# PSUM constants, a shared bank for the state product, and spread ordering copies in an attention, routing and expert kernel

## The chip, the cores and the metric

The kernel runs on one core of a Trainium2 chip. The metric is device time in microseconds: the median of three runs before the change is 863.5 us, from 861.35 to 866.65. An execution that the hardware profiler recorded took 862.23 us.

## The reference

Three layers follow one another; the output of each is the input of the next.

```python
# 1: gated linear attention, B=4, heads 8, sequence 768, head size 48
f = 1.0 / (1.0 + np.exp(-f_logit))
for t in range(S):
    state = f[:, :, t, :, None] * state + np.einsum('bhd,bhe->bhde', k[:, :, t], v[:, :, t])
    y[:, :, t] = np.einsum('bhd,bhde->bhe', q[:, :, t], state)
# 2: 3072 tokens x 384; 8 experts, 384 tokens each, given out in order of the logits x @ w_gate
out[mask] = np.maximum(x[mask] @ w1[e], 0.0) @ w2[e]          # F = 1024
# 3: dense layer, 2048 wide
h = x @ w_in
out = (h * np.clip(h + 3.0, 0.0, 6.0) / 6.0) @ w_out
```

The weights w_in and w_out of the third layer arrive as 64-bit floating point numbers; the kernel reads them as pairs of 32-bit words.

## The kernel before, in words

**Attention** runs on 24 chunks of 128 tokens (`NCH`). Three chunks make a unit of 384 tokens (`U`), eight units in all (`NU`). For a unit, the rows of f, k and q are loaded, put in order per head pair by three copies each (`reorder`: f and k on ScalarE, with the tanh in f's copy; q on GpSimd), and transposed on TensorE into one of three PSUM banks `pT` (line 82). ScalarE turns a transposed f into the forget factors `ff` (line 86). VectorE makes from these two running products by scans: P forward (line 94, whose second stream `m0` restarts the product at each chunk) and S backward (line 92). k times S is `kh` (line 99), q times P is `qt` (line 106). The products at chunk ends, held at a least value of 2^-60, are `pc` (line 96).

A unit has twelve such transposed groups (`ORD`, four head pairs times f, k, q). They are made one unit ahead, four in each chunk (`tg(0)` to `tg(3)`), and `group` puts VectorE's work of one group behind that of the group before. The order of all queues is the order in which the loop over j at the end of `attention` issues things; no scheduler moves them. In an iteration the loop issues:

1. `tg(0)`, then the logits and output of the chunk before (`l_mm`, line 196, into the one bank `pM`), one deferred ScalarE copy (`one`), `tg(1)`;
2. the state's part of the output (`y_mm` part 0, line 164), the scores of the next chunk (`a_mm`, line 136, into the banks pA0 and pA1), their two copies out on ScalarE (`a_ev`, line 141) and masks on GpSimd (line 142);
3. the rest of the output (line 170), then the key-value product (`kv_mm`, line 182, into its own bank `pK`), which VectorE adds to the state (line 189) at the end of the next group;
4. `tg(2)`, the transposed keys of the next chunk (`kt_mm`, line 149, into `pM`, copied out on ScalarE at line 150), `tg(3)`.

PSUM has eight banks, all taken: three pT, pA0, pA1, pM, pY, pK. Chunks are counted here by their scores: chunk n begins with the first matmul of line 136 for it.

`refill` is called in each third chunk: for f its three copies are issued at once, for k they go into a list (`byact`), from which `one` takes one at a time.

Between VectorE's steps of a group, the loop takes a step of the preparation of w_in and w_out (`narrowed`): for each piece of 128x512 words, ScalarE takes the absolute high word (line 904), VectorE holds it at a least value of 2^-15 (line 914), shifts it (916), puts in sign and exponent (918) and joins the low word (921, written over the loaded words `pw`). ScalarE rounds the result to the high half `wih` (691), GpSimd subtracts for the low half `wil` (692). A piece two further on is then fetched into the `pw` buffer that this frees.

**Routing and experts.** A search over the logits picks each expert's tokens; its first steps lie among the last chunks. Each expert's 384 tokens go through both later layers in three matmul passes per product (lines 695 to 697). In the last matmuls `l4` of an expert (k is its number, f the slice of 128 of the 2048 hidden values, t one of three groups of 128 tokens) the three results are finished one after the other, scaled on ScalarE (868) and stored by an indirect DMA that GpSimd issues (870).

Of the kernel before, what the change touches and what calls it, by code (L numbers as in the profile page):

```python
# [17 lines left out]
def attention(tc, q,k,v,f,wg, x_dram, lg, ident, pmin, ranges, prep, setup, spin):  # L18
    nc=tc.nc
    ctx=ExitStack()  # L20
    with ctx:
# [10 lines left out]
        m0=cs.tile([128,U],F32,name="m0")  # L32
        nc.vector.memset(m0,0.0)
        nc.vector.memset(m0.rearrange("p (c t) -> p c t",t=C)[:,:,0:1],1.0)
        m1=cs.tile([128,2,U],F32,name="m1"); nc.vector.memset(m1,0.0)
# [33 lines left out]
        def tgroup(u,p,nm):  # L69
# [14 lines left out]
            if nm=='f':  # L84
# [11 lines left out]
                return (ops+[lambda: V.tensor_scalar(PC[u][:,pp],ends(P2),PMIN,None,op0=OP.max)],  # L96
# [46 lines left out]
        def kt_mm(j):  # L143
# [3 lines left out]
            pk=ps.tile([128,NP,128],F32,name="pM",bufs=MB)  # L147
# [26 lines left out]
        def kv_mm(j):  # L174
# [3 lines left out]
            bank=ps.tile([128,512],F32,name="pK")  # L178
            pk=bank[:,:NP*D].rearrange("p (a d) -> p a d",a=NP)
# [12 lines left out]
        def l_mm(j):  # L192
            W=2*D+8
            px=ps.tile([128,512],F32,name="pM" if j<NCH-1 else "pK",bufs=MB)[:,:NP*W].rearrange("p (a e) -> p a e",a=NP)
# [20 lines left out]
        def warm(n):  # L215

            t=ps.tile([128,512],F32,name="pK")
            for _ in range(n): nc.tensor.matmul(t[:,:128],ident,ident,start=True,stop=True)
# [8 lines left out]
        def refill(u,nm):  # L227
            if u<NU:
                if nm=='k':
# [10 lines left out]
        for nm in 'fkq': refill(1,nm)  # L240
        one()
# [4 lines left out]
        for j in range(-1,NCH+1):  # L246
# [11 lines left out]
            one()  # L258
# [3 lines left out]
            if ti==2: refill(tu+1,'f')  # L262
# [6 lines left out]
            if j>=0: kv_mm(j)  # L269
            tg(2)  # L270
            one()
# [3 lines left out]
            if ti==2: refill(tu+1,'k'); one()  # L275
# [59 lines left out]
class Routing:  # L335
# [3 lines left out]
    def constants(s):  # L339
# [36 lines left out]
        G.iota(w,pattern=[[-1,4]],base=4,channel_multiplier=1)  # L376
        nc.vector.tensor_scalar(w,w,3,None,op0=OP.bitwise_and)
# [3 lines left out]
        G.iota(w,pattern=[[-1,128]],base=128,channel_multiplier=1)  # L381
        nc.vector.tensor_scalar(w,w,31,None,op0=OP.bitwise_and)
# [318 lines left out]
class Experts:  # L701
# [90 lines left out]
    def ffn_(s,k):  # L792
# [61 lines left out]
        for f in range(14):  # L854
# [9 lines left out]
        for t in range(3):  # L864
            l4(14,t); yield
# [12 lines left out]
def gla_moe_ffn(tc,q,k,v,f_logit,moe_w_gate,moe_w1,moe_w2,moe2_w_in,moe2_w_out,out):  # L878
    nc=tc.nc
    with ExitStack() as ctx:  # L880
# [9 lines left out]
        def narrowed(pool,jobs,W,work,places,PW=None):  # L890
# [17 lines left out]
            for i in range(len(jobs)):  # L908
                yield
                r=got[i]  # L910
                if words:
                    V=nc.vector
                    lw,hw=got[i][:,:,0],got[i][:,:,1]; m=mag[i]; t=m.bitcast(U32)
                    V.tensor_scalar(m,m,2.0**-15,None,op0=OP.max)
# [6 lines left out]
                    V.scalar_tensor_tensor(lw,lw,29,t,op0=OP.logical_shift_right,op1=OP.bitwise_or)  # L921
                    r=lw.bitcast(F32)
                hi,lo=places(i)
                if W!=DM:
                    split_raw(nc,r,hi,lo,nc.gpsimd)
                    fetch(i+2)
# [47 lines left out]
        def both(*gens):  # L974
            for g in gens: yield from g
# [133 lines left out]
```

## Time and profile before

| | us |
|---|---|
| median of three runs | 863.5 (861.35 to 866.65) |
| the profiled execution | 862.23 |
| its span, first to last instruction | 860.5 |
| TensorE busy (matmuls), share of the span | 816.0, 95% |
| VectorE busy | 564.4, 66% |
| ScalarE busy | 381.4, 44% |
| GpSimd busy | 155.7, 18% |
| attention's last matmuls start | 179.25 |
| last matmul starts | 848.88 |

[...] Where a row names a releaser, the engine was idle before the instruction until that releaser ended. On TensorE neighbouring matmuls overlap, so the pace is read from start to start. Engines: PE is TensorE, PEld its weight loads, DVE VectorE, ACT ScalarE, POOL GpSimd, SP the queue of most DMAs.

### The profile page before, as it was taken

The numbers are of one execution on the slowest core, as the hardware profiler recorded it, in microseconds if no ns is written. First come the engines' busy times: TensorE is split into PE (matmuls) and PEld (weight loads), VectorE is DVE, ScalarE is ACT, GpSimd is POOL, SyncE is SP. The second block draws the span as 40 slices with busy tenths as digits, with TensorE's granted clock in tenths as the row PEclk, the third lists the DMA queues.
The fourth block names the chain that finished last, engine by engine and source line by source line (L and its number), as shares of the span: only waits on it lengthen the run. The fifth ranks groups of instructions, "written<-read, shape, count | busy, mean of one in ns | idle before, by whom it ended". The sixth has DMA issues, their size and how long they took to land.

```text
span 860.5 us, 15930 instructions
## 1 busy us (share of the span) xinstructions
PE 816.0 (95%) x6062; PEld 778.5 (90%) x6062; DVE 564.4 (66%) x1491; ACT 381.4 (44%) x768; POOL 155.7 (18%) x233
## 2 busy tenths in 40 slices
PE   7999899888998899999999999999999999999994
PEld 6878788777987899999999999999999999999994
DVE  7999999767879846855674676657665522642431
ACT  5776677524345424441453254245415432641431
POOL 5665565302000200110101100300110020000001
PEclk9999999996999999999999999999999999999997
DMA  8776776256002301211211121202211230210000
GB/s 240 191 208 174 195 194 162 86 212 211 1 1 74 111 19 62 87 56 37 74 56 53 50 65 47 83 22 71 90 30 47 58 100 1 74 40 26 1 1 32
DMA packets 77157, 71.91 MB, mean 84 GB/s; under 512 B 29200, under 2 KB 65040, under 8 KB 77072
## 3 DMA queue, kind: packets, MB, share of 16 engines
q1 hardware_dynamic: 74000, 61.37, 24.7%
q0 software_dynamic: 3072, 9.44, 3.4%
q8 instruction: 49, 0.80, 0.4%
q14 instruction: 36, 0.29, 0.1%
HBM read 61.35 MB, written 9.44 MB: 82 GB/s over the span
## 4 chain that ended last, share of the span: by engine, by line
PE 54%; DVE 11%; issue 10%; ACT 3%; DMA 1%; POOL 1%; SPq 0%; POOLq 0%; DVEq 0%; ACTq 0%
PE pF L695 9%; PE acc L695 9%; PE pF L696 8%; PE pF L697 8%; PE acc L697 8%; PE acc L696 8%; DVE ga L838 2%; DVE hl L841 2%; ACT hh L840 1%; DVE w1l L744 1%; ACT ga L837 1%; DMA xh<-in_moe_w_dram 1%; POOL out_dram L870 1%; PE pF L782 1%; DVE q_ge L473 1%
## 5 line engine op out<-in xcount | busy, mean ns | idle before, releaser
L838 DVE SCALAR_TENSOR_TENSOR ga<-ga,pF 128x384 f32<-128x384 f32 x128 | 70.8, 553 | 97.5 <-ACT ga L837 97.1
L695 PE MATMUL pF<-xh,wih 128*128 128x384 f32 x384 | 131.0, 341 | 0.0
L696 PE MATMUL pF<-xh,wil 128*128 128x384 f32 x384 | 129.4, 337 | 0.0
L697 PE MATMUL pF<-xl,wih 128*128 128x384 f32 x384 | 129.3, 337 | 0.0
L837 ACT ACTIVATE ga<-pF,three 128x384 f32<-128x384 f32 x128 | 74.3, 580 | 90.7 <-PE pF L697 83.9
L840 ACT CAST hh<-ga 128x384 fp32r<-128x384 f32 x128 | 65.8, 514 | 101.4 <-DVE ga L838 101.4
L695 PE MATMUL acc<-wo,hh 128*128 128x384 f32 x288 | 100.8, 350 | 0.0
L696 PE MATMUL acc<-wo,hl 128*128 128x384 f32 x288 | 97.4, 338 | 0.1
L697 PE MATMUL acc<-wo,hh 128*128 128x384 f32 x288 | 97.4, 338 | 0.0
L870 POOL DMA_INDIRECT out_dram<-ga,q_ids x24 | 23.9, 997 | 395.3 <-ACT ga L868 392.0
L841 DVE TENSOR_TENSOR hl<-ga,hh 128x384 fp32r<-128x384 f32 x128 | 71.3, 557 | 31.2 <-ACT hh L840 28.0
L803 ACT ACTIVATE hh<-pF 128x384 fp32r<-128x384 f32 x64 | 31.5, 492 | 130.3 <-PE pF L697 125.4
L804 DVE SCALAR_TENSOR_TENSOR hl<-pF,hh 128x384 fp32r<-128x384 f32 x64 | 35.5, 555 | 73.8 <-ACT hh L803 73.5
L695 PEld LDWEIGHTS pF<-xh,wih 128*128 128x128 f32 x384 | 72.3, 188 | 0.2 <-issue 0.2
L696 PEld LDWEIGHTS pF<-xh,wil 128*128 128x128 f32 x384 | 72.2, 188 | 0.0
L697 PEld LDWEIGHTS pF<-xl,wih 128*128 128x128 f32 x384 | 72.1, 188 | 0.0
L695 PE MATMUL pF<-xh,w1h 128*128 128x384 f32 x192 | 67.7, 353 | 0.6 <-ACT xh L773 0.6
L695 PE MATMUL acc<-hh,w2h 128*128 128x384 f32 x192 | 65.9, 343 | 0.0
L696 PE MATMUL pF<-xh,w1l 128*128 128x384 f32 x192 | 65.8, 343 | 0.0
L697 PE MATMUL pF<-xl,w1h 128*128 128x384 f32 x192 | 65.7, 342 | 0.0
L697 PE MATMUL acc<-hl,w2h 128*128 128x384 f32 x192 | 64.5, 336 | 0.1
L761 POOL DMA_INDIRECT xg<-x_dram,q_ids x24 | 24.4, 1017 | 220.8 <-PE pF L697 111.5
(303 smaller groups left out, 1839.4 us busy)
## 6 DMA issues: line engine op xcount, KB each, us to landing
wst<-in_moe_w_dram SPq DMA_DIRECT2D x58, 192.0 KB, 2.4
wst<-in_moe_w_dram SPq DMA_DIRECT2D x42, 256.0 KB, 2.7
pw<-in_moe_w_in_dram SPq DMA_DIRECT2D x12, 512.0 KB, 3.8
v<-in_v_dram SPq DMA_DIRECT2D x24, 192.0 KB, 4.8
x_dram<-y SPq DMA_DIRECT2D x24, 192.0 KB, 4.2
wo<-in_moe_w_out_dram SPq DMA_DIRECT2D x12, 384.0 KB, 8.0
fr<-in_f_logit_dram SPq DMA_DIRECT2D x7, 576.0 KB, 5.2
kr<-in_k_dram SPq DMA_DIRECT2D x7, 576.0 KB, 5.5
```

The source lines that it names most:

```text
L473: V.scalar_tensor_tensor(ge[:,c0:c1],x[:,c0:c1,None].to_broadcast([128,c1-c0,32]),base[:,0:1],grid[:,None,:].to_broadcast([128,c1-c0,32]), ...
L695: nc.tensor.matmul(out, ahi, bhi, start=start, stop=False)
L696: nc.tensor.matmul(out, alo, bhi, start=False, stop=False)
L697: nc.tensor.matmul(out, ahi, blo, start=False, stop=stop)
L761: nc.gpsimd.indirect_dma_start(out=xg[:,h],out_offset=None,in_=s.x,in_offset=bass.IndirectOffsetOnAxis(ap=ids[:,h:h+1],axis=0))
L803: nc.scalar.activation(hh,p,AF.Relu)
L804: s.defer(2,lambda: nc.vector.scalar_tensor_tensor(hl,p,0.0,hh.bitcast(F32),op0=OP.max,op1=OP.subtract))
L837: nc.scalar.activation(a,p,AF.Relu,bias=s.three[:,0:1])
L838: late(f,1,lambda: nc.vector.scalar_tensor_tensor(g,a,6.0,p,op0=OP.min,op1=OP.mult))
L840: late(f,1,lambda: nc.scalar.copy(gh,g))
L841: late(f,3,lambda: nc.vector.tensor_tensor(out=gl,in0=g,in1=gh.bitcast(F32),op=OP.subtract))
L870: st=nc.gpsimd.indirect_dma_start(out=s.out,out_offset=bass.IndirectOffsetOnAxis(ap=ids[:,t:t+1],axis=0),in_=o,in_offset=None)
```

## The change

1. The bank `pK` goes to constants (`held`): m0, the least value 2^-60 and the least value 2^-15 lie there in PSUM. The P scan reads m0 from it; the two maxima with a constant become maxima of two tensors, the second a column of the bank read again and again.
2. The key-value product is written into pA0; the warming matmuls at the start into pY; the last chunk's logits into pT. The transposed keys of chunks 22 and 23 go to pT (23 has none).
3. f's three copies are issued one at a time from the second chunk of a unit on, k's copies two at the unit's last chunk and one in the next.
4. A joined word of w_in is written into its scratch `pm` and not over `pw`, and the next fetch is issued ahead of the low half's subtraction.
5. Two constants of the routing are made in two steps, so that VectorE's part is issued an iteration after GpSimd's.
6. In the last expert, f = 13 of the last matmuls moves into the loop over t.

```diff
--- before
+++ after
@@ -29,9 +29,10 @@
             nc.vector.memset(t[:,:,:,:,48:],1.0 if nm=='f' else 0.0)
             perm[nm]=t
         half=cs.tile([128,1],F32,name="half"); nc.vector.memset(half,0.5)
-        m0=cs.tile([128,U],F32,name="m0")
-        nc.vector.memset(m0,0.0)
+        held=ps.tile([128,512],F32,name="pC"); m0=held[:,:U]
+        nc.vector.memset(held[:,:U],0.0); nc.vector.memset(held[:,U:U+1],PMIN); nc.vector.memset(held[:,U+1:],2.0**-15)
         nc.vector.memset(m0.rearrange("p (c t) -> p c t",t=C)[:,:,0:1],1.0)
+        least=held[:,U:U+1,None].to_broadcast([128,2,3]); normal.append(held[:,U+1:U+2])
         m1=cs.tile([128,2,U],F32,name="m1"); nc.vector.memset(m1,0.0)
         SW=cs.tile([128,NP,2*D+8],F32,name="sw"); nc.vector.memset(SW,0.0)
         for s in range(2):
@@ -93,7 +94,7 @@
                 SF[u,p]=suffix
                 ops=[lambda: V.tensor_tensor_scan(P,m0,ff[:,:U],1.0,op0=OP.max,op1=OP.mult)]
                 if p%2==0: return ops,[]
-                return (ops+[lambda: V.tensor_scalar(PC[u][:,pp],ends(P2),PMIN,None,op0=OP.max)],
+                return (ops+[lambda: V.tensor_tensor(out=PC[u][:,pp],in0=ends(P2),in1=least,op=OP.max)],
                         [lambda: V.reciprocal(ends(m1),PC[u][:,pp]),SF[u,p-1]])
             elif nm=='k':
                 return [lambda: nc.vector.tensor_mul(KH[u][:,p],pf,SS[u,p])],[]
@@ -144,7 +145,8 @@
             u,c=divmod(j,3)
             if j%6==5: return
             kt=wk.tile([128,4,2,64],F32,name="kt")
-            pk=ps.tile([128,NP,128],F32,name="pM",bufs=MB)
+            idle=j>NCH-3
+            pk=ps.tile([128,NP,128],F32,name="pT" if idle else "pM",bufs=PB if idle else MB)
             for p in range(NP):
                 nc.tensor.transpose(pk[:,p],KH[u][:,p,c*C:(c+1)*C],ident)
             nc.scalar.copy(kt.rearrange("p a s d -> p a (s d)"),pk)
@@ -175,8 +177,7 @@
             u,c=divmod(j,3); first=j%6==0
             if j%6==5 or j>=NCH: return
             vr=raw['v',u]
-            bank=ps.tile([128,512],F32,name="pK")
-            pk=bank[:,:NP*D].rearrange("p (a d) -> p a d",a=NP)
+            pk=ps.tile([128,512],F32,name="pA0")[:,:NP*D].rearrange("p (a d) -> p a d",a=NP)
             for p in range(NP):
                 for s in range(2):
                     nc.tensor.matmul(pk[64*s:64*s+64,p],KT[j][:,p,s],vr[:,c,2*p+s,:D],start=True,stop=True)
@@ -191,7 +192,7 @@
             late.append(update)
         def l_mm(j):
             W=2*D+8
-            px=ps.tile([128,512],F32,name="pM" if j<NCH-1 else "pK",bufs=MB)[:,:NP*W].rearrange("p (a e) -> p a e",a=NP)
+            px=ps.tile([128,512],F32,name="pM" if j<NCH-1 else "pT",bufs=MB if j<NCH-1 else PB)[:,:NP*W].rearrange("p (a e) -> p a e",a=NP)
             for p in range(NP):
                 nc.tensor.matmul(px[:,p],YT[j][:,p],SW[:,p],start=True,stop=True)
             y=wk.tile([128,NP,2*D],F32,name="y")
@@ -214,7 +215,7 @@
         WARM=(4,1,8,0); RF,RK=2,4
         def warm(n):
 
-            t=ps.tile([128,512],F32,name="pK")
+            t=ps.tile([128,512],F32,name="pY")
             for _ in range(n): nc.tensor.matmul(t[:,:128],ident,ident,start=True,stop=True)
         warm(WARM[0])
         for i,(p,nm) in enumerate(ORD):
@@ -226,7 +227,7 @@
         later=[]
         def refill(u,nm):
             if u<NU:
-                if nm=='k':
+                if nm in 'fk':
                     for r in range(3): byact.append(lambda r=r: reorder(u,nm,r))
                     if u+1<NU: byact.append(lambda: later.append(lambda: load(u+1,nm)))
                     return
@@ -237,8 +238,10 @@
 
             if byact: byact.pop(0)()
             if len(byact)==1: byact.pop(0)()
-        for nm in 'fkq': refill(1,nm)
-        one()
+        refill(1,'f')
+        while byact: one()
+        for nm in 'kq': refill(1,nm)
+        one(); one()
         next(prep)
         while later: later.pop(0)()
         constants,early=setup()
@@ -255,11 +258,10 @@
             if j==NCH: spin(lambda: ps.tile([128,384],F32,name="pT",bufs=PB),TAIL[0])
             tg(0)
             if 0<=j-1<NCH: l_mm(j-1)
-            one()
+            if ti!=1: one()
             if j==NCH: spin(lambda: ps.tile([128,384],F32,name="pT",bufs=PB),TAIL[1])
             tg(1)
             while later: later.pop(0)()
-            if ti==2: refill(tu+1,'f')
             if 0<=j<NCH: y_mm(j,0)
             if j+1<NCH:
                 a_mm(j+1)
@@ -267,12 +269,14 @@
                 a_ev(j+1,1)
             if 0<=j<NCH: y_mm(j,1)
             if j>=0: kv_mm(j)
+            if ti==1: refill(tu+1,'f')
             tg(2)
-            one()
+            if ti==1: one()
             if j+1<NCH: kt_mm(j+1)
             if ti==2: refill(tu+1,'q')
             tg(3)
-            if ti==2: refill(tu+1,'k'); one()
+            if ti==1: one()
+            if ti==2: refill(tu+1,'k'); one(); one()
             if j>=0: next(constants,None)
             if j>=NCH-4: next(ranges,None)
             if j in (17,22,24): next(early)
@@ -374,11 +378,13 @@
         yield
         s.mask=c("mask",[128,4],F32); w=s.t("mi",[128,4],I32)
         G.iota(w,pattern=[[-1,4]],base=4,channel_multiplier=1)
+        yield
         nc.vector.tensor_scalar(w,w,3,None,op0=OP.bitwise_and)
         nc.vector.tensor_scalar(s.mask,w,0.0,None,op0=OP.is_equal)
         yield
...
@@ -851,7 +857,8 @@
             yield
         for t in range(3):
             o=s.pa.tile([128,DM],F32,name=f"acc{t}"); oacc.append(o)
-        for f in range(14):
+        close=13 if k==E-1 else 14
+        for f in range(close):
             for t in range(3):
                 l4(f,t); yield
             if f+4<16:
@@ -862,7 +869,8 @@
                     yield
         ids=s.rt.ids[k]
         for t in range(3):
-            l4(14,t); yield
+            for f in range(close,15):
+                l4(f,t); yield
             l4(15,t)
             o=s.act.tile([128,DM],F32,name="ga",bufs=3)
             nc.scalar.activation(o,oacc[t],AF.Copy,scale=1.0/6.0)
@@ -911,19 +919,21 @@
                 if words:
                     V=nc.vector
                     lw,hw=got[i][:,:,0],got[i][:,:,1]; m=mag[i]; t=m.bitcast(U32)
-                    V.tensor_scalar(m,m,2.0**-15,None,op0=OP.max)
+                    V.tensor_tensor(out=m,in0=m,in1=normal[0].to_broadcast([128,W]),op=OP.max)
                     yield
                     V.tensor_scalar(t,t,3,0x3ffffff8,op0=OP.logical_shift_left,op1=OP.bitwise_and)
                     yield
                     V.scalar_tensor_tensor(t,hw,0xC0000000,t,op0=OP.bitwise_and,op1=OP.bitwise_or)
                     yield
                     absolute(i+1)
-                    V.scalar_tensor_tensor(lw,lw,29,t,op0=OP.logical_shift_right,op1=OP.bitwise_or)
-                    r=lw.bitcast(F32)
+                    if W!=DM:
+                        V.scalar_tensor_tensor(t,lw,29,t,op0=OP.logical_shift_right,op1=OP.bitwise_or); r=m
+                    else:
+                        V.scalar_tensor_tensor(lw,lw,29,t,op0=OP.logical_shift_right,op1=OP.bitwise_or); r=lw.bitcast(F32)
                 hi,lo=places(i)
                 if W!=DM:
+                    fetch(i+2)
                     split_raw(nc,r,hi,lo,nc.gpsimd)
-                    fetch(i+2)
                 else:
                     nc.scalar.copy(hi,r)
                     yield
```

Three places in the queues. **ScalarE, from chunk 4's output copy to the next unit's first f.** In the names, pA_789 and pA_790 (793 and 794 after) are chunk 5's banks pA0 and pA1. Before:

```order
L172 COPY yt<-pY 128x512
L150 COPY kt<-pM 128x512
L201 COPY y<-pM 128x384
L904 ACTIVATE pm<-pw 128x512
L691 CAST wih<-pw 128x512
L65 ACTIVATE pmf<-fr 128x8x48 x3
L141 COPY am<-pA_789 128x512
L141 COPY am<-pA_790 128x512
L172 COPY yt<-pY 128x512
L66 COPY pmk<-kr 128x8x48
L86 ACTIVATE ff_121<-pT,half 128x384
L201 COPY y<-pM 128x384
```

After:

```order
L174 COPY yt<-pY 128x512
L66 ACTIVATE pmf<-fr 128x8x48
L152 COPY kt<-pM 128x512
L66 ACTIVATE pmf<-fr 128x8x48
L202 COPY y<-pM 128x384
L66 ACTIVATE pmf<-fr 128x8x48
L912 ACTIVATE pm<-pw 128x512
L697 CAST wih<-pm 128x512
L142 COPY am<-pA_793 128x512
L142 COPY am<-pA_794 128x512
L174 COPY yt<-pY 128x512
L67 COPY pmk<-kr 128x8x48 x2
```

The three f copies between the cast and the score copies are spread ahead of the cast, and two k copies follow chunk 5's output where one did.

**TensorE, from the end of a chunk's scores to the next transposes** (St is the state, kt the transposed keys). Before:

```order
L136 MATMUL pA_789<-qt,kh_116 128x128
L136 MATMUL pA_790<-qt,kh_116 128x128
L170 MATMUL pY<-am,v_113 64x128 x8
L182 MATMUL pK<-v_113,kt 64x48 x8
L82 MATMUL pT<-ident,pmq 128x128 x3
```

After:

```order
L137 MATMUL pA_793<-qt,kh_118 128x128
L137 MATMUL pA_794<-qt,kh_118 128x128
L172 MATMUL pY<-am,v_115 64x128 x8
L183 MATMUL pA_818<-v_115,kt 64x48 x8
L83 MATMUL pT<-ident,pmq 128x128 x3
```

The order is the same; pA_818 is a new tile in the bank of pA_793, which ScalarE must have copied out before.

**TensorE, keys of chunk 22 and logits of chunk 21.** Before:

```order
L182 MATMUL pK<-v_113,kt 64x48 x8
L149 MATMUL pM<-ident,kh_116 128x128 x4
L989 MATMUL pT<-ident,q_cnt 3x128
L196 MATMUL pM<-sw,yt 128x104 x4
L164 MATMUL pY<-qt,St_117 64x128 x8
```

After:

```order
L183 MATMUL pA_2493<-v_115,kt 64x48 x8
L151 MATMUL pT<-ident,kh_118 128x128 x4
L999 MATMUL pT<-ident,q_cnt 3x128
L197 MATMUL pM<-sw,yt 128x104 x4
L166 MATMUL pY<-qt,St_119 64x128 x8
```

The keys leave pM, so the logits behind them no longer share a bank with them.

## Rows read from the trace of the kernel before

**Rows 1.** Busy time by stretch: length, each engine's busy us (instructions), granted clock, DMA.

```profile
24.40:160.20 135.80, 127.47 (x1647) 111.17 (x1646) 129.60 (x245) 93.52 (x187) 82.91 (x125) 1.00 0.67 181
```

**Rows 2.** Timeline of TensorE: start, us, line, operation, tiles; three matmul groups of one chunk.

```profile
64.94 1.16 PE L136 MATMUL pA<-qt,kh 64*128 64x128 f32 x16
...
66.95 0.62 PE L182 MATMUL pK<-v,kt 128*64 128x48 f32 x16
...
71.58 1.16 PE L136 MATMUL pA<-qt,kh 64*128 64x128 f32 x16
```

**Rows 3.** Waits in the first 190 us: who waited for whom, total us, times, longest.

```profile
ACT wih L691 <- DVE pw L921: 10.6, 8, 2.4
...
PE pT L82 <- POOL pmq L67: 3.0, 4, 1.2
PE pT L82 <- ACT pmk L66: 2.5, 3, 1.1
...
PE pT L82 <- ACT am L141: 1.6, 3, 0.8
...
PE pT L82 <- DVE kh L99: 1.3, 1, 1.3
```

**Rows 4.** VectorE by line and shape, first 190 us: busy us, mean ns, idle before.

```profile
L94 DVE TENSOR_TENSOR_SCAN P<-m,ff 128x384 f32<-128x384 f32 x32 | 35.5, 1117 | 5.7 <-ACT ff L86 5.7
L92 DVE TENSOR_TENSOR_SCAN S<-ff,m 128x384 f32<-128x384 f32 x32 | 32.4, 1017 | 0.1
L99 DVE TENSOR_TENSOR kh<-pT,S 128x384 f32<-128x384 f32 x28 | 15.2, 544 | 0.1
...
L914 DVE TENSOR_SCALAR pm<-pm 128x512 f32<-128x512 f32 x12 | 10.9, 905 | 0.0
...
L96 DVE TENSOR_SCALAR pc<-P 128x6 f32<-128x6 f32 x16 | 6.3, 395 | 0.3
...
L97 DVE RECIPROCAL m<-pc 128x6 f32<-128x6 f32 x16 | 3.0, 185 | 0.2
...
L930 DVE TENSOR_TENSOR wol<-pw,woh 128x384 fp32r<-128x384 f32 x4 | 2.2, 550 | 1.5 <-ACT woh L928 1.5
```

**Rows 5.** Timeline of VectorE, two single instructions.

```profile
53.60 1.51 DVE L914 TENSOR_SCALAR pm<-pm 128x512 f32<-128x512 f32 x1
...
66.08 0.94 DVE L94 TENSOR_TENSOR_SCAN P<-m,ff 128x384 f32<-128x384 f32 x1
```

**Rows 6.** Timeline of GpSimd at the first of them.

```profile
53.52 1.31 POOL L692 TENSOR_TENSOR wil<-pw,wih 128x512 fp32r<-128x512 f32 x1 [3.24 <-ACT wih L691]
```

**Rows 7.** Timeline of ScalarE: score copies of four chunks, and copies ahead.

```profile
26.27 1.07 ACT L141 COPY am<-pA 128x512 f32<-128x512 f32 x2
...
66.18 1.07 ACT L141 COPY am<-pA 128x512 f32<-128x512 f32 x2
...
115.03 1.35 ACT L65 ACTIVATE pmf<-fr 128x384 f32<-128x384 f32 x3
116.28 1.04 ACT L141 COPY am<-pA 128x512 f32<-128x512 f32 x2
...
155.79 1.07 ACT L141 COPY am<-pA 128x512 f32<-128x512 f32 x2
```

**Rows 8.** Timeline of TensorE: key-value products of the three late chunks.

```profile
26.40 0.62 PE L182 MATMUL pK<-v,kt 128*64 128x48 f32 x16
...
114.99 0.62 PE L182 MATMUL pK<-v,kt 128*64 128x48 f32 x16
...
155.88 0.62 PE L182 MATMUL pK<-v,kt 128*64 128x48 f32 x16
```

**Rows 9.** Timeline of TensorE: logits of chunk 21.

```profile
170.96 1.14 PE L196 MATMUL pM<-sw,yt 128*128 128x104 f32 x8 [1.35 <-ACT kt L150]
```

**Rows 10.** Timeline of GpSimd: first and last of the three final stores.

```profile
848.00 0.97 POOL L870 DMA_INDIRECT out_dram<-ga,q_ids  x1 [71.52 <-ACT ga L868]
...
850.55 0.97 POOL L870 DMA_INDIRECT out_dram<-ga,q_ids  x1 [0.21 <-issue]
```

More of the change, by code (lines that the diff above doesn't have):

```diff
@@ L16, with attention @@
 PMIN=2.0**-60; PB=3; MB=1
-def attention(tc, q,k,v,f,wg, x_dram, lg, ident, pmin, ranges, prep, setup, spin):
+def attention(tc, q,k,v,f,wg, x_dram, lg, ident, pmin, ranges, prep, setup, spin, normal):
     nc=tc.nc
@@ L381, in constants @@
         G.iota(w,pattern=[[-1,128]],base=128,channel_multiplier=1)
+        yield
         nc.vector.tensor_scalar(w,w,31,None,op0=OP.bitwise_and)
@@ L936, in prep_in @@
                             lambda i: (wih[:,i//4,cc(i)],wil[:,i//4,cc(i)]))
-        woh={}; wol={}
+        woh={}; wol={}; normal=[]
         def prep_out(pool,wr,g0,g1,PW=DM):
@@ L1007, in gla_moe_ffn @@
         with tc.tile_pool(name="prep",bufs=1) as pi:
-            attention(tc,q,k,v,f_logit,moe_w_gate,x_dram,lg,ident,pmin,ranges,both(prep_in(pi),prep_out(pi,wr0,0,NOUT,512)),lambda: (rt.constants(),p0),rt.spin)
+            attention(tc,q,k,v,f_logit,moe_w_gate,x_dram,lg,ident,pmin,ranges,both(prep_in(pi),prep_out(pi,wr0,0,NOUT,512)),lambda: (rt.constants(),p0),rt.spin,normal)
         wr=ctx.enter_context(tc.tile_pool(name="wout",bufs=1))
```

## The prediction

> **What bounds the kernel now.** I read the table of stretches first. In the steady part of attention, 24.4 to 160.2 us, TensorE is busy for 127.5 of 135.8 us and VectorE for 129.6 [rows 1]: two engines at 94 and 95%, so neither can be relieved alone for more than the other leaves free. TensorE's timeline shows its pace. A chunk with all its parts, from the first score matmul at 64.94 to the next at 71.58, takes 6.64 us with matmuls back to back [rows 2]; five of the twenty chunks take just that. So TensorE sets the floor, and what can be won in this stretch is at most its idle time, 135.8 - 127.5 = 8.3 us. Behind attention the routing, the weights and the experts follow one another by data, and the change touches only the last expert's last matmuls there: time won in attention moves everything behind it forward, and nothing else is won but a little at the end.
>
> Next, whom TensorE waits for: 3.0 us for GpSimd's q copies, 2.5 for ScalarE's k copies, 1.6 for its score copies and 1.3 for VectorE's kh, all at the transposes into pT [rows 3]. In its queue ScalarE has ahead of such score copies a cast that waited 10.6 us in all for VectorE's joined words [rows 3], so I read the 1.6 and the 1.3 alike as VectorE's lag: 2.9 us.
>
> Then why VectorE is so full. The groups by shape show the same scan twice, but P (two inputs in SBUF) at a mean of 1117 ns and S at 1017; the tiny 128x6 maximum at 395 ns beside a reciprocal of the same size at 185; and the 128x512 maximum at 905 [rows 4]. Single instructions explain it: the maximum at 53.60 takes 1.51 us, while GpSimd's subtraction starts at 53.52 and ends at 54.83; a P scan that meets nothing takes 0.94 [rows 5, 6]. [...] The product kh, with one input in PSUM, shows none of that: 28 of them with a mean of 544 [rows 4].
>
> **The change, part by part.**
>
> *PSUM constants.* Three kinds leave the contention, as one input of each now lies in PSUM.
> - 32 P scans, 1117 to 945 ns: 5.5 us of VectorE. Bounds: 940 (the free one) and 1117 (no relief); I take 945, as kh shows what one PSUM input does.
> - 16 small maxima, 395 to 185 (the reciprocal): 3.4 us; bounds 3.4 and 0.
> - 12 word maxima become two-input instructions. kh's 544 ns for 384 columns, scaled to 512, gives 0.73 us: 12 x (0.905 - 0.73) = 2.1 us saved. Of the 1.51 us of the one at 53.60, 0.28 lay behind GpSimd's end, so unhindered they take perhaps 0.35 today: if the stalls stayed, the new form would lose 12 x 0.38 = 4.6. These are the bounds; I take the gain, as kh meets no stall. Four more, of 384 columns, lose at worst 0.38 x 3/4 each: 1.1, which I count.
>
> Sum: 9.9 us off VectorE, most of it out of the 129.6, so VectorE falls to some 121 and TensorE alone is the bound. The extra memsets at the start lie ahead of waits for ScalarE's f that the P scans show (5.7 us) [rows 4]: nothing.
>
> [...]
>
> *ScalarE's copies.* Before, three f copies of 1.35 us together stand right ahead of the score copies in each third chunk [rows 7]; now one does, and the other two come earlier. The third k copy moves ahead of the unit's first f eviction. The 2.5 us of TensorE waiting for k copies goes: that copy is now issued about two thirds of a chunk earlier. What it delays is the f eviction behind it, by a copy (1.35 / 3 = 0.45 us), and so perhaps the score copies, in the three such chunks that have a state product: 0 to 1.4 us. I take 0, as ScalarE is busy for only 93.5 of the 135.8 us [rows 1].
>
> *The state product's bank.* This is the wait added. The key-value matmuls now write into pA0, so they wait for ScalarE's first score copy out of it; queued behind them on TensorE are the next transposes and so everything. Where ScalarE is prompt the copy ends 66.18 + 0.58 = 66.76, and the matmuls start at 66.95 [rows 2, 7]: free by 0.2 us. In ten of the twenty chunks it is late: first 26.27 + 0.58 against 26.40 (0.45), at worst 116.28 + 0.58 against 114.99 (1.9), last 155.79 + 0.58 against 155.88 (0.5) [rows 7, 8]; the ten sum to 9.6 us. Bounds 0 and 9.6. In five late third chunks two f copies, up to 0.9 us, are gone from in front of the pair: some 4 off. The rest follows VectorE's lag (ScalarE's cast there waits for a joined word), and shrinks with its 10 us. I take 2.5 us. On the other side the next scores wait for VectorE's update of the state out of pA0: the matmuls start at 66.95, the next scores at 71.58 [rows 2], 4.6 us for one small addition, so nothing.
>
> *Words joined in scratch, refetch first.* Same four VectorE steps; the refetch no longer stands behind GpSimd's subtraction, and the SP queue behind it moves up. TensorE waits for none of it directly, so I cost it at nothing; if a word came late, ScalarE's cast would stand in front of the score copies, as above.
>
> *Last chunk's keys in pT.* The logit matmuls at 170.96 waited 1.35 us for the key copy in the shared pM bank [rows 9]. That wait goes, and the chain ran through it: 1.3 us.
>
> *Last expert's order.* Token tile 0 ends two l4 triplets, some 1 us, earlier. The three stores leave at 848.00 and, 1.27 apart, the last at 850.55 [rows 10], the last late only because the queue before it was full. With tiles 1.56 us apart the last starts when its data is there, near 850.0: 0.5 us.
>
> **The sum.** Steady part: 2.5 (k copies) + 2.9 (VectorE's lag) + about 1 of the 2.9 us that is left of its 8.3 us idle, less 2.5 for the new wait: 3.9. The 3.0 of waiting for q copies falls mostly before 24.4 us; the stalls that VectorE loses GpSimd loses too, and I take not quite half: 1.3. Then 1.3 for the keys and 0.5 for the end. Together 7.0: the profiled execution's 862.2 becomes 855.2. The median of the runs shown is 863.5, 1.3 above it; for a median I say 855.5.
>
> **The rivals.**
>
> 1. *The new wait decides* (slower). If ScalarE stays as late as today, the ten late chunks each hold TensorE at the state product: 9.6 us. Its condition is that VectorE's stalls stay, so that ScalarE's casts come as late and the word maxima lose their 4.6. Against that stand the k copies less what the wait absorbs (1), the keys (1.3) and the end (0.5): 862.2 + 9.6 + 4.6 - 2.8 = 873.6; with some of the f copies' relief, 870. It makes the kernel slower from 2.8 us of remaining lateness upwards. For it: ScalarE's prompt copies clear by only 0.2 us. Against: most of the lateness is caused by what the change removes. 8%, of which 5% lie over 1% slower.
> 2. *The stalls move.* GpSimd's work stays, and S scans, whose 1017 against 945 shows 2.3 us of the same stalls, and word steps meet it instead. VectorE keeps half its 10 us and stays level with TensorE: the 3.9 us that the sum has from VectorE (2.9 + 1) halve, and the new wait, which follows VectorE, is 3.5 and not 2.5: 862.2 - 7.0 + 2.0 + 1.0 = 858.2. Longer S scans than today's would take more. For it: GpSimd is busy for 82.9 of the 135.8 us [rows 1]. Against: S scans run as closely behind GpSimd's work today and mostly miss it. 12%.
> 3. *A PSUM input costs something*, up to the 0.05 us by which like products differ among themselves: 64 x 0.05 = 3.2 us on VectorE, a third of its relief. A third of the 3.9 and 0.8 more of the new wait: 855.2 + 1.3 + 0.8 = 857.3. Against it stand kh and wol. [...] 6%.
> 4. *TensorE runs free.* The new wait is nearly nothing and the stretch reaches its floor: 8.3 less 1 for rounding at the ends, plus 2.5 at the start, 1.3 and 0.5: 851. 17%.
>
> The forecast itself has 57%, with a spread from 852 to 859 by the bounds of its terms.
>
> **How the numbers follow.** One per cent, about what a measurement here can tell from no change, is 8.6 us: faster means under 854.9. Rival 4 and 45% of the forecast are under it: 0.17 + 0.26 = 0.43. Five of rival 1's 8% lie above 872.1: 0.05. The rest is 0.52. For the range, rival 4's price with another 3 us for a start that gains in full gives 848; above, rivals 2 and 3 and the runs' spread of 3 us about their median give 863, with rival 1 outside.
>
> **What would show it.** P scans at 0.94 to 0.97 and 128x6 maxima under 0.2 us, without a tail: right on the contention; S scans or word steps with longer means: rival 2. No wait of transposes for k copies. The state product waiting for ScalarE's score copy by 2 to 3 us in total; near 9, rival 1. The logit matmuls of chunk 21 without their 1.35 us. TensorE's busy share from 24 us to attention's end at 97% or more, and that end 6 to 7 us earlier; the last store near 0.5 us closer to the last matmul. The forecast is wrong if the attention stretch shortens by less than 3 us, or if the time from attention's end to the last matmul changes by more than 2.

## The result, and the profile after

The changed kernel takes 854.11 us (median of 4 runs, 851.42 to 854.97) against 862.9 us (median of 4, 861.35 to 866.65): a ratio of 0.988, with a 95% interval from 0.9856 to 0.9904. The forecast was 855.5, within 848 to 863. The profiled execution of the changed kernel took 853.68 us, with a span of 852.0.

I cut both spans at the same marks: the first scores of chunks 1, 21 and 23, the first matmul of the experts, the first of the second expert, the start of the last l4 matmul, and that of the last store.

| stretch | before, us | after, us | won | forecast |
|---|---|---|---|---|
| start to chunk 1 | 24.38 | 21.72 | 2.66 | 1.3 |
| chunk 1 to 21 (steady) | 135.86 | 129.58 | 6.28 | 3.9 |
| chunk 21 to 23 | 12.81 | 11.20 | 1.61 | 1.3 |
| chunk 23 to the first expert | 31.70 | 32.02 | -0.32 | 0 |
| first expert | 95.48 | 97.28 | -1.80 | 0 |
| second expert to the last l4 | 548.65 | 548.82 | -0.17 | 0 |
| last l4 to the last store | 1.67 | 1.14 | 0.53 | 0.5 |
| last store to the end | 9.96 | 10.21 | -0.25 | 0 |
| sum | 860.51 | 851.97 | 8.54 | 7.0 |

Attention gave 10.6 us where 6.5 were forecast, and the first expert took 1.8 of them back. The table of stretches answers to [rows 1] (length, then busy us of TensorE, its weight loads, VectorE, ScalarE and GpSimd, granted clock, DMA share, GB/s), the steady stretch first, then chunks 21 to 23 and the first expert:

```profile
21.70:151.30 129.60, 126.10 (x1647) 111.09 (x1646) 120.49 (x245) 94.23 (x187) 68.63 (x125) 1.00 0.69 190
151.30:162.50 11.20, 10.47 (x155) 9.31 (x153) 7.67 (x22) 7.24 (x15) 3.84 (x7) 1.00 0.25 72
194.50:291.80 97.30, 87.96 (x493) 83.13 (x493) 80.65 (x242) 43.42 (x90) 4.54 (x7) 0.93 0.17 53
```

In the steady stretch VectorE is down from 129.6 busy us to 120.5, TensorE is busy for 126.1 of 129.6, 97.3%, and GpSimd's 125 instructions take 68.6 us where they took 82.9. VectorE's groups by shape in the first 190 us answer to [rows 4]:

```profile
L93 DVE TENSOR_TENSOR_SCAN S<-ff,m 128x384 f32<-128x384 f32 x32 | 32.8, 1030 | 0.1
L95 DVE TENSOR_TENSOR_SCAN P<-pC,ff 128x384 f32<-128x384 f32 x32 | 29.9, 944 | 3.7 <-ACT ff L87 3.7
L922 DVE TENSOR_TENSOR pm<-pm,pC 128x512 f32<-128x512 f32 x12 | 8.0, 664 | 0.0
L924 DVE TENSOR_SCALAR pm<-pm 128x512 uint32<-128x512 uint32 x12 | 5.7, 479 | 0.0
L97 DVE TENSOR_TENSOR pc<-P,pC 128x6 f32<-128x6 f32 x16 | 2.6, 160 | 0.3
L922 DVE TENSOR_TENSOR wol<-wol,pC 128x384 f32<-128x384 f32 x4 | 2.2, 541 | 0.0
```

The P scans fell from a mean of 1117 ns to 944, the small maxima from 395 to 160, the word maxima from 905 to 664; the S scans, both inputs still in SBUF, stayed (1017, now 1030). The means hide a spread (shortest, median and longest in ns), for small and word maxima before, and for word maxima after:

```profile
L96 DVE TENSOR_SCALAR pc<-P x16: 170/420/597, 8.1 to 151.1; 128x6 f32<-128x6 f32 x16
L914 DVE TENSOR_SCALAR pm<-pm x12: 393/789/1518, 29.7 to 135.7; 128x512 f32<-128x512 f32 x12
...
L922 DVE TENSOR_TENSOR pm<-pm,pC x12: 655/662/680, 26.8 to 127.1; 128x512 f32<-128x512 f32 x12
```

So the long ones are gone, but the shortest word maximum took less in the old form (393) than it does now (655). The waits of the same time answer to [rows 3]:

```profile
ACT wih L697 <- DVE pm L930: 3.2, 6, 1.2
PE pM L197 <- ACT kt L152: 2.3, 5, 0.8
PE pA L183 <- ACT am L142: 1.3, 2, 1.0
```

ScalarE's cast waits 3.2 us for VectorE's words, not 10.6. In the steady stretch (not at the start) TensorE no longer waits for k copies, for kh, or for score copies ahead of transposes; the second row is the logits waiting for a key copy. The third is the new wait, of the state product for ScalarE's score copy, in single instructions of TensorE (a state product, a prompt one, the late one, and the logits of chunk 21, which answer to [rows 2, 8, 9]):

```profile
24.23 0.67 PE L183 MATMUL pA<-v,kt 128*64 128x48 f32 x16 [0.33 <-ACT am L142]
...
101.20 0.62 PE L183 MATMUL pA<-v,kt 128*64 128x48 f32 x16
...
140.26 0.67 PE L183 MATMUL pA<-v,kt 128*64 128x48 f32 x16 [0.96 <-ACT am L142]
...
160.51 1.04 PE L197 MATMUL pM<-sw,yt 128*128 128x104 f32 x8
```

With a third of 0.13 us at 76.77, too short for the table of waits, the new wait sums to 1.4 us, of 9.6 that rival 1 allowed for. Its longest has a cause of its own, seen on ScalarE:

```profile
139.15 0.58 ACT L87 ACTIVATE ff<-pT,half 128x384 f32<-128x384 f32 x1 [1.78 <-DVE S L93]
139.63 1.06 ACT L142 COPY am<-pA 128x512 f32<-128x512 f32 x2
```

ff stands ahead of the score copies and waits for an S scan, and on VectorE the routing's first step (five instructions from 135.90 on, the longest 1.00 us at 136.18, line 453) lies ahead of that scan. The logits at 160.51 show no wait. The final stores, on GpSimd, answer to [rows 10]:

```profile
838.65 0.97 POOL L878 DMA_INDIRECT out_dram<-ga,q_ids  x1 [70.47 <-ACT ga L876]
...
841.76 0.97 POOL L878 DMA_INDIRECT out_dram<-ga,q_ids  x1 [0.48 <-issue]
```

The three lie 1.56 us apart and no longer 1.27, and the last starts 1.14 us behind the last l4 matmul (840.62), not 1.67.

### The profile page after: what moved, and what is told of

It reads as the page before. It is cut to its first block, busy times and chain, and to the rows that moved or that the text cites. A ratio compares the mean times of both kernels' runs of the same rounds, so it can differ in the third digit from the quotient of the medians.

```text
span 852.0 us, 15921 instructions
## 1 busy us (share of the span) xinstructions
PE 815.0 (96%) x6062; PEld 778.8 (91%) x6062; DVE 555.1 (65%) x1493; ACT 381.5 (45%) x768; POOL 140.4 (16%) x233
## 4 chain that ended last, share of the span: by engine, by line
PE 66%; DVE 15%; issue 11%; ACT 4%; DMA 2%; POOL 1%; SPq 0%; POOLq 0%; DVEq 0%; ACTq 0%
PE acc L701 9%; PE pF L701 8%; PE acc L703 8%; PE pF L703 8%; PE pF L702 8%; PE acc L702 8%; PE pT L83 3%; PE pA L137 2%; PE pM L197 2%; PE pY L166 2%; PE pY L172 2%; DVE ga L844 2%; DVE hl L847 2%; DMA qr<-in_q_dram 1%; ACT hh L846 1%
## 5 line engine op out<-in xcount | busy, mean ns | idle before, releaser
L702 PE MATMUL acc<-hh,w2l 128*128 128x384 f32 x192 | 64.5, 336 | 0.0
```

What stands on the lines that cost most here:

```text
L702: nc.tensor.matmul(out, alo, bhi, start=False, stop=False)
```

## The experiments

Each kernel but e6 is the changed one with the edit shown; e6 starts from the kernel before. All on one scale (steady: chunk 1 to 21; busy and idle time are of that stretch, from one profiled execution each; the ratio is to runs of the kernel before made beside them, and "95%" is its interval):

| kernel | steady | VectorE busy | TensorE idle | chunk 1 at | 21 to 23 | time, us | ratio, 95% |
|---|---|---|---|---|---|---|---|
| before | 135.86 | 129.6 | 8.3 | 24.38 | 12.81 | 862.9 | 1 |
| changed | 129.58 | 120.5 | 3.5 | 21.72 | 11.20 | 854.11 | 0.9856 to 0.9904 |
| e1 constants in SBUF | 137.36, with a spell at a granted clock of 0.50 | 132.4 | 8.2 | 24.39 | 11.20 | 862.38 | 0.9957 to 0.9996 |
| e5 the same, own bank | 136.22 | 133.2 | 8.9 | 24.09 | 11.20 | 861.96 | 0.9958 to 0.9990 |
| e6 constants alone | 134.47 | 120.7 | 7.6 | 23.02 | 13.02 | 860.0 | 0.9937 to 0.9974 |
| e2 scans' constant back | 131.64 | 125.5 | 4.6 | 24.61 | 11.20 | 856.34 | 0.9888 to 0.9944 |
| e3 maxima back | 131.22 | 125.0 | 4.7 | 23.32 | 11.20 | 855.33 | 0.9853 to 0.9929 |
| e4 copies back | 132.40 | 120.5 | 5.6 | 22.65 | 11.20 | 855.61 | 0.9867 to 0.9939 |
| e7 words back | 129.99 | | | 22.19 | 11.40 | 852.64 | 0.9835 to 0.9906 |
| e11 masks twice | 138.84 | 128.7 | 11.5 | 22.18 | 13.10 | 863.26 | one run |
| e9 ends back | 129.58 | | | 22.11 | 12.81 | 855.38 | one run |
| e13 changed, again | 129.58 | 120.5 | 3.5 | 22.91 | 11.20 | 852.78 | 0.9855 to 0.9899 |
| e8 chunk 21's keys too | 129.55 | | | 22.85 | 10.87 | 853.04 | 0.9856 to 0.9898 |
| e12 and routing later | 128.43 | | | 22.25 | 12.26 | 853.06 | 0.9864 to 0.9904 |

The theory: the constants free VectorE of GpSimd's stalls, and TensorE's idle time goes with its lag. Against it: the stalls only move (rival 2), or the gain comes from ScalarE's order and the words, or the new wait (rival 1) eats a part.

**e1, the constants back in SBUF**, the maxima again with a number; all else as changed.

```diff
-        held=ps.tile([128,512],F32,name="pC"); m0=held[:,:U]
+        m0=cs.tile([128,U],F32,name="m0"); nc.vector.memset(m0,0.0)
...
-                    V.tensor_tensor(out=m,in0=m,in1=normal[0].to_broadcast([128,W]),op=OP.max)
+                    V.tensor_scalar(m,m,2.0**-15,None,op0=OP.max)
```

> The changed kernel with the constants back in SBUF and as immediates, the state product still in pA0. Landmark: start of chunk 23's scores, 173.05 us before the change, 162.50 after. Theory 1 (GpSimd's stalls of VectorE were the bound, the PSUM constants removed them): P scans again at a mean of 1.05 to 1.12 us, the landmark back by 5 to 7 us to about 168.5, the time about 860. Theory 2 (the spread copies and the early refetch brought the gain): scans as slow, but the landmark at 163 to 164 and the time within 1.5 us of the changed kernel's 854.

7.8 us of the steady stretch come back, more than the change had won there. Some 1.7 of them are a spell of a lower clock that this execution met (shown under e5; an estimate: at a granted clock of 0.50, half of its 3.4 us), so without it the constants would account for some 6.1. VectorE's groups by shape:

```profile
L93 DVE TENSOR_TENSOR_SCAN P<-m,ff 128x384 f32<-128x384 f32 x32 | 35.1, 1106 | 4.7 <-ACT ff L85 4.7
L91 DVE TENSOR_TENSOR_SCAN S<-ff,m 128x384 f32<-128x384 f32 x32 | 34.5, 1083 | 0.1
L920 DVE TENSOR_SCALAR pm<-pm 128x512 f32<-128x512 f32 x12 | 10.6, 880 | 0.0
L95 DVE TENSOR_SCALAR pc<-P 128x6 f32<-128x6 f32 x16 | 6.8, 422 | 0.3
```

and whom TensorE waited for from chunk 1 to 21 (total, times, longest):

```profile
PE pA L181 <- ACT am L140: 4.9, 8, 1.9
...
PE pM L195 <- ACT kt L150: 1.6, 4, 0.8
...
PE pT L81 <- DVE kh L98: 1.2, 3, 0.8
```

The old durations are back, and the state product waits 4.9 us: the new wait follows VectorE's lag, as the prediction had it, but even here it is half of rival 1's 9.6.

**e2, only the scans' constant back in SBUF**, and **e3, only the two maxima back**. They part the 7.8 us.

```diff
-        held=ps.tile([128,512],F32,name="pC"); m0=held[:,:U]
+        held=ps.tile([128,512],F32,name="pC")
...
+        m0=cs.tile([128,U],F32,name="m0"); nc.vector.memset(m0,0.0)
```

> The changed kernel with m0 alone back in SBUF, both maxima still against PSUM columns. Theory 1, weighted by VectorE's time lost (P scans 5.5 of 11): the landmark (chunk 23's scores) 2.5 to 3.5 us later than 162.50. If only the short maxima mattered: within 0.5 us. Theory 2: within 0.5 us.

```diff
-                return (ops+[lambda: V.tensor_tensor(out=PC[u][:,pp],in0=ends(P2),in1=least,op=OP.max)],
+                return (ops+[lambda: V.tensor_scalar(PC[u][:,pp],ends(P2),PMIN,None,op0=OP.max)],
...
-                    V.tensor_tensor(out=m,in0=m,in1=normal[0].to_broadcast([128,W]),op=OP.max)
+                    V.tensor_scalar(m,m,2.0**-15,None,op0=OP.max)
```

> The changed kernel with m0 in PSUM and both maxima again against immediates (one SBUF input). Theory 1: maxima of 128x6 near 0.39 us and of 128x512 near 0.9 us in the mean again, 5 us of VectorE, the landmark 2 to 3.5 us later than 162.50. If the scans carried all of it: within 0.5 us. Theory 2: within 0.5 us.

The scans alone cost 2.1 us of the stretch when they go back (P at 1079 ns), the maxima 1.6 (128x6 at 379 ns): 3.7 together, of some 6.1 that both cost without e1's clock spell. VectorE is busy for 125 us in each, half of its way back to 132.4, and TensorE's idle time is 4.6 and 4.7 us, a quarter of its way from 3.5 to 8.2: the room that one half leaves VectorE hides a part of the other's cost.

**e5, constants back and the state product in its own bank**: e1's edit and this one, so the copies, the words, the routing's two steps and the ends without PSUM constants.

```diff
-            pk=ps.tile([128,512],F32,name="pA0")[:,:NP*D].rearrange("p (a d) -> p a d",a=NP)
+            pk=ps.tile([128,512],F32,name="pK")[:,:NP*D].rearrange("p (a d) -> p a d",a=NP)
```

> As the first of these (constants in SBUF), with the state product in a bank of its own as before the change: the order of copies, the refetch, the keys' bank and the end stay new. Against the first it prices the shared bank while VectorE's stalls stay. Theory 1 with the forecast's sizes: landmark 2 to 4 us earlier than the first. Rival of the forecast (the new wait decides where the stalls stay): 5 to 9 us earlier. If the wait is absorbed by later waits: under 1 us.

In the steady stretch ScalarE's new order, with the words and the routing's two steps, is worth nothing by itself: 136.22 against 135.86 before. No k copy is waited for, but VectorE is busy for 133.2 of the 136.2 us, and TensorE meets its lag at the transposes behind kh, 4.9 us in five waits, three of which are:

```profile
76.37 0.55 PE L81 MATMUL pT<-ident,pmf 128*128 128x128 f32 x3 [1.15 <-DVE kh L98]
97.58 0.55 PE L81 MATMUL pT<-ident,pmf 128*128 128x128 f32 x3 [1.43 <-DVE kh L98]
...
137.35 0.55 PE L81 MATMUL pT<-ident,pmf 128*128 128x128 f32 x3 [0.93 <-DVE kh L98]
```

Between e1 and e5 lies the shared bank alone. Its waits record 4.9 us in e1, and yet TensorE is idle there for 8.2 us and here for 8.9: without them 3.7 us more of waiting for kh (4.9 here, 1.2 in e1) stand behind in TensorE's queue for the same lag. That e1's stretch is 1.1 us longer lies in busy time, 129.2 us against 127.3, and in the clock. Of the two, e1 alone has a spell of a lower clock in this stretch (granted 0.50 for 3.41 us; e5's mean is 1.00). The whole stretch, five microseconds with the longest of the new waits (1.93 us at 149.34), and the spell behind them, in e1, and the whole stretch in e5:

```profile
24.39:161.75 137.36, 129.19 (x1648) 112.52 (x1648) 132.38 (x245) 93.70 (x187) 81.71 (x125) 0.99 0.65 179
145.79:150.79 5.00, 3.07 (x52) 2.65 (x49) 4.86 (x11) 2.98 (x6) 1.44 (x2) 1.00 0.58 133
150.79:154.20 3.41, 3.41 (x19) 3.32 (x17) 3.37 (x10) 0.88 (x2) 0.57 (x1) 0.50 0.00 0
...
24.09:160.31 136.22, 127.31 (x1647) 111.22 (x1647) 133.23 (x245) 93.23 (x187) 82.42 (x125) 1.00 0.66 180
```

So these executions show no idle time that the shared bank adds. Whether the new wait brought the spell on or this execution met it by chance stays open.

**e4, the copies in the old order**, constants in PSUM.

```diff
-                if nm in 'fk':
+                if nm=='k':
...
+            if ti==2: refill(tu+1,'f')
...
-            if ti==1: refill(tu+1,'f')
...
-            if ti==2: refill(tu+1,'k'); one(); one()
+            if ti==2: refill(tu+1,'k'); one()
```

> The changed kernel with ScalarE's f and k copies in the order of before, all else new. Theory (with VectorE relieved TensorE is the bound, so ScalarE's order now counts; it did not while VectorE stalled): transposes wait for k copies again and the state product waits for late score copies; chunk 23's scores 2 to 4 us later than 162.50. Rival (the spread is worth nothing in either state): within 0.5 us.

With VectorE relieved (120.5 busy) the copies are worth 2.8 us. One wait for a k copy is back, and the state product waits 3.1 us in all, not 1.4:

```profile
61.40 0.33 PE L83 MATMUL pT<-ident,pmk 128*128 128x128 f32 x1 [1.12 <-ACT pmk L67]
```

**e6, the kernel before with the constants in PSUM** and the state product in pA0: copies, words, yields, keys and ends undone (the diffs of e4, e7 and e9, with the setup's added yields gone, which is the routing's two steps).

> The kernel before with the PSUM constants and the shared bank that they need, nothing else of the change. Theory: chunk 23's scores at 165 to 168, against 173.05 before, the state product waiting for score copies by 1.5 to 4 us in all; the time near 857 to 859. Rival 1 of the forecast (the new wait decides, as ScalarE's copies are in the old order): 5 us or more of waits at the state product, landmark after 169.5.

VectorE is relieved in full (120.7), yet the stretch wins only 1.4 us, and chunk 23's scores come at 170.50, later than expected: TensorE is idle for 7.6, as its waits show.

```profile
PE pA L182 <- ACT am L142: 3.7, 6, 0.9
...
PE pT L83 <- ACT pmk L67: 2.4, 2, 1.2
```

Constants alone 1.4 (with the shared bank that they need), everything else alone nothing, both 6.3: each part uncovers the wait that the other removes.

**e7, the words joined in place and the refetch behind the subtraction.**

```diff
-                    if W!=DM:
-                        V.scalar_tensor_tensor(t,lw,29,t,op0=OP.logical_shift_right,op1=OP.bitwise_or); r=m
...
-                    fetch(i+2)
                     split_raw(nc,r,hi,lo,nc.gpsimd)
+                    fetch(i+2)
```

> The changed kernel with w_in's words joined over the loaded ones and the refetch behind GpSimd's subtraction, as before. Forecast: costs nothing, so chunk 23's scores within 0.5 us of 162.50. Rival (late words hold ScalarE's casts, and with them the score copies and the state product): 1 to 3 us later, with ScalarE waiting for loads of words.

0.4 us in the steady stretch, 0.2 in the next, and a time that can't be told from the changed kernel's: small, as it was costed. Chunk 23's scores come 1.1 us later than in the changed kernel's profile, but 0.5 of that lie ahead of chunk 1. The routing's two steps were not undone by themselves: no run prices them.

**e11, GpSimd's masks of the scores computed twice**: the second affine_select changes no value, and only GpSimd has more work.

```diff
             nc.gpsimd.affine_select(out=am,in_=am,pattern=[[0,NP],[1,C]],compare_op=OP.is_ge,fill=0.0,base=0,channel_multiplier=-1)
+            nc.gpsimd.affine_select(out=am,in_=am,pattern=[[0,NP],[1,C]],compare_op=OP.is_ge,fill=0.0,base=0,channel_multiplier=-1)
```

> The changed kernel with every one of GpSimd's 48 masks done twice, the second changing nothing. Theory (a VectorE instruction stands still behind GpSimd only if its inputs are all in SBUF): P scans stay at 0.944 us and the 128x6 maxima at 0.16, S scans rise from 1.03 to 1.1 or more, the 128x512 shifts too. Rival (the long scans came from something else than GpSimd): S scans within 0.02 us of 1.03. GpSimd's added 30 us also delay the masks themselves, so the landmark may be later in either case.

```profile
L93 DVE TENSOR_TENSOR_SCAN S<-ff,m 128x384 f32<-128x384 f32 x32 | 36.3, 1139 | 0.1
L95 DVE TENSOR_TENSOR_SCAN P<-pC,ff 128x384 f32<-128x384 f32 x32 | 29.9, 944 | 3.0 <-ACT ff L87 2.9
...
L925 DVE TENSOR_SCALAR pm<-pm 128x512 uint32<-128x512 uint32 x12 | 7.9, 658 | 0.0
```

This is the plainest reading of the mechanism. With 36 us more of GpSimd (104.6 against 68.6) the S scans go from 1030 to 1139 ns and the shifts from 479 to 658, while P stays at 944, and both maxima where they were (158 and 662). So the groups shown that lengthen have all their inputs in SBUF, and those with an input in PSUM don't lengthen. But inputs in SBUF alone do not settle it: the reciprocals of 128x6 took 188 ns in both runs, and an S scan of the kernel before took 0.95 us although a subtraction of GpSimd (2.04 us, where the one at 53.52 took 1.31) began with it:

```profile
144.22 0.95 DVE L92 TENSOR_TENSOR_SCAN S<-ff,m 128x384 f32<-128x384 f32 x1
...
144.22 2.04 POOL L692 TENSOR_TENSOR wil<-pw,wih 128x512 fp32r<-128x512 f32 x1
```

The 9.3 us of the steady stretch are not VectorE's alone, since TensorE waits 6.8 us for the new state here, which GpSimd multiplies behind its masks.

**e9, the ends as before**: chunk 22's and 23's keys through pM, and the last expert closing at 14.

```diff
-            idle=j>NCH-3
+            idle=False
...
-        close=13 if k==E-1 else 14
+        close=14
```

> The changed kernel with chunk 22's keys back in the bank of the logits and the last expert's last matmuls in the order of before. Forecast's terms: from chunk 21's scores to chunk 23's 1.3 us longer than 11.20, with a wait of the logits for the key copy; the last store 0.5 us further behind the last matmul than 1.14. Rival: both hidden, under 0.3 us each.

Chunk 21 to 23 takes 12.81 us again, and the last l4 to the last store 1.67. On TensorE:

```profile
162.42 1.14 PE L197 MATMUL pM<-sw,yt 128*128 128x104 f32 x8 [1.35 <-ACT kt L152]
```

So 1.6 us belong to the keys and 0.5 to the order of the last expert.

**e13, the changed kernel once more**, unedited, for the first expert's 1.8 us.

> The changed kernel once more, as the partner of the version above on the same chip and for a second record of the first expert: 853 to 855. If the half-clock spells in the first expert fall by chance, this record has them elsewhere and its first expert differs from 97.28 us by a microsecond or more while attention repeats to 0.3 us; if they follow from the order of the work, they repeat.

The steady stretch is the same to 0.01 us, but the first expert takes 94.33 us and not 97.28, and chunk 23 to the last l4 676.22 and not 678.12 (before: 675.83). Two pieces of the first expert (columns as above), in the changed kernel's first profile

```profile
208.00:212.00 4.00, 2.20 (x13) 1.91 (x12) 3.32 (x10) 1.45 (x3) 0.00 (x0) 0.98 0.00 0
212.00:216.00 4.00, 4.00 (x16) 3.69 (x15) 2.73 (x9) 1.00 (x2) 0.00 (x0) 0.59 0.02 4
...
283.00:287.00 4.00, 2.40 (x17) 1.73 (x16) 3.66 (x9) 2.38 (x6) 0.00 (x0) 0.99 0.15 49
287.00:290.40 3.40, 3.06 (x11) 2.59 (x11) 2.20 (x8) 1.85 (x4) 1.09 (x2) 0.51 0.44 130
```

and in this one:

```profile
208.00:212.00 4.00, 4.00 (x29) 3.66 (x27) 3.44 (x7) 0.63 (x3) 0.00 (x0) 1.00 0.00 0
212.00:216.00 4.00, 2.75 (x17) 2.48 (x17) 3.30 (x11) 1.77 (x5) 0.00 (x0) 1.00 0.01 4
...
283.00:287.00 4.00, 2.61 (x18) 1.94 (x16) 3.77 (x8) 2.46 (x7) 0.00 (x0) 1.00 0.16 49
287.00:290.40 3.40, 2.74 (x17) 2.29 (x17) 2.40 (x8) 2.29 (x6) 1.09 (x2) 1.00 0.39 119
```

In the first profile the granted clock drops twice more in this stretch (to 0.59 and 0.51 in the pieces shown; its mean is 0.93, and 0.96 here), each time right behind a piece in which TensorE was busy for 2.2 to 2.4 of 4 us; here it stays at 1.00 in the pieces shown. Both have a drop between 266 and 270 (0.57 in each), behind a piece with 1.21 and 1.31 of 4. So the expert's 1.8 us are not the price of the change but of which drops an execution meets. What decides a single drop stays open.

**e8, chunk 21's keys in pT too**, and **e12, that with the routing's first step at chunk 20**, off the place where the 0.96 us wait arose.

```diff
-            idle=j>NCH-3
+            idle=j>NCH-4
```

> The changed kernel with chunk 21's keys in pT as well, the routing step left after chunk 17. If the version with both lost on the routing step what it won on it, this one keeps its 0.73 us: from chunk 21's scores to chunk 23's 10.5 us against 11.20, the steady part at 129.58 as it was, the time within noise of the changed kernel. If the keys' wait was hidden by what follows: 11.2.

```diff
-            if j in (17,22,24): next(early)
+            if j in (20,22,24): next(early)
```

> A version meant to beat the changed kernel: chunk 21's keys go to pT too (its logits waited 0.73 us for the shared bank), and the first routing step is issued after chunk 20 and not 17, where its 2 us on VectorE stood between two S scans and held ScalarE's f, the score copies and then the state product (0.96 us). Expected: chunk 23's scores 1.2 to 2 us earlier than 162.50, the time near 852.5. If the routing step is then needed on the way out of attention: what is won is given back between chunk 23 and the first expert.

Neither beats the changed kernel. In e8 the logits' 0.73 us at the end of the stretch go, but 0.60 come back two steps later, and only 0.3 us are won of the 0.7 expected. In e12 the steady stretch wins 1.15 us and chunk 21 to 23 gives 1.06 back, in two waits on TensorE:

```profile
160.03 1.11 PE L197 MATMUL pM<-sw,yt 128*128 128x104 f32 x8 [0.97 <-DVE lg L199]
...
161.93 1.09 PE L166 MATMUL pY<-qt,St 64*64 64x128 f32 x16 [0.79 <-POOL St L191]
```

## Why the prediction was right, and where it was not

- *VectorE is freed of GpSimd's stalls*: right, and to size. P at 944 ns (945 forecast), the small maxima at 160 (185), the word maxima at 664 (730). By the same groups as the forecast's 9.9 us that is 11.4 (four maxima of 384 columns lost 0.8); VectorE's busy time in the steady stretch falls by 9.1. e11 shows it by itself: with 36 us more of GpSimd S rises by 109 ns and P by none.
- *Rival 2, the stalls move*: refuted. S rose by 13 ns, 0.4 us over 32, and by 1 in e13 (1018).
- *Rival 3, a PSUM input costs something*: not seen. P from PSUM takes what the shortest P from SBUF took (0.94), and wol's maximum with an input in PSUM takes 541 ns beside 550 for the remainder in SBUF alone. What does cost is the change of form: from a maximum with a number to one of two tensors, 393 to 655 ns for the shortest of 512 columns, which the forecast had counted in (0.35 to 0.73).
- *Rival 1, the new wait*: it exists and follows VectorE's lag, but was overpriced. Its 9.6 us counted each late score copy in full, when later waits in the same queue already held most of that lag: e1 records 4.9 us of it and is idle no longer than e5, which has none.
- *The steady stretch, 3.9 us*: mis-sized; 6.3 measured. The new wait took 1.4 and not 2.5; in all 3.5 us of TensorE's 8.3 of idle time are left, the new wait among them, where the sum came to 4.4. The other 1.4 us are busy time: 127.5 before, 126.1 now, for the same 1647 matmuls, and the sum had no term for it: it took the busy time as a fixed floor. What shortens it no run shows. The working also added terms as if each stood alone. e5 and e6 show that they don't: apart they give nothing and 1.4, together 6.3. Copies first uncover VectorE's lag, constants first uncover ScalarE's.
- *The start, 1.3 us*: 2.7 in the profiled execution, part of it luck. The kernels with all constants in PSUM and the new copies begin chunk 1 between 21.72 and 22.91, so 1.5 to 2.7 against 24.38. Before, TensorE waited for q copies four times, 1.6 us near 7 to 8 us and 1.4 near 21 and 22. The later two are gone in the changed kernel and in e13, and back in e2, which has the scans' constant alone in SBUF: that is the change's part, about what I forecast. Of the earlier, 0.5 us are left in the changed kernel's profile and 1.7 in e13's; what moves the start by a microsecond between two executions of one kernel stays open.
- *Keys 1.3 and last store 0.5*: right (1.6 and 0.53; e9 gives both back).
- *Time won in attention moves everything behind it forward, and nothing else changes*: this step failed in the profiled execution by 2.3 us, over the 2 that the prediction allowed. By e13 the order of the work is not the cause; the first expert varies between two executions of one kernel by as much (97.28 us at a mean granted clock of 0.93, 94.33 at 0.96). The prediction had taken that stretch from one execution as fixed.

That the total was within 1.4 us of the forecast is in part luck: the last point took back part of what the steady stretch and the start won beyond their terms. In e13's profile the first expert takes nothing back, and that execution took 852.78 us, 2.7 under the forecast.

## What to carry to other kernels

When two engines are both nearly full, cost a change of several parts as a whole: remove one wait and ask which engine is late next at that very place, since parts that are worth nothing alone can be worth most of the gain together. Here small constants kept in PSUM, in a bank freed for them, took the VectorE instructions that read them out of GpSimd's way (P 1117 to 944 ns, and 944 still with e11's 36 us more of GpSimd). For the scans and the small maxima that cost nothing (944 and 160 ns, beside 940 and 170 for the shortest before); the word maxima lost their shorter form (shortest 393 ns, now 655) and still gained in the mean, 905 to 664, since most of them had been longer than that. Before two profiles are compared, their granted clock is: one spell of 3.4 us at 0.50 made e1's stretch look as if the shared bank cost 1.1. And a recorded wait is not its price: see what stands behind it in the same queue for the same cause.

## What the runs showed that I had not expected

- A maximum of 6 columns took 395 ns when it had only an SBUF input and a number, and 160 as one with two tensors, one in PSUM. The shortest in the old form took 170, so its time was more than half stall.
- GpSimd gained more than VectorE (9.1 us): its masks of the scores went from a mean of 809 ns to 668, and its busy time in the steady stretch from 82.9 us to 68.6.
- One kernel's first expert took 94.33 us in one execution and 97.28 in another, with attention the same to 0.01 us.
